# Padding the attention matmuls to 128 columns and fixing a finely interleaved order of all steps

## Chip, cores, metric

One core of a Trainium2 chip. The metric is the device time of one execution in microseconds. Each median below is that of three to seven executions of a kernel in one call. The calls ran on different chips; each had the kernel before beside the others, with a median of 174.8 to 175.2 us in every one. Engines: PE is the matrix engine, PEld its weight loads, DVE the vector engine, ACT the scalar engine, POOL the general-purpose one, SP the one that issues most DMAs.

Every run carries a label, fast or slow. A program on one core gets "slow" when it is over 1.5% above the fastest run of the same kernel in its call. Medians take all runs.

## The reference

Attention with polynomial features, then a Fourier mix with an MLP, in four batches:

```python
phi(x) = outer(S1 @ x, S2 @ x).reshape(64)      # q, k: (4, 4, 1088, 32) -> 64 features
kv  = einsum('bhsf,bhsd->bhfd', phi(k), v);  z = phi(k).sum(s)
x   = (phi(q) @ kv) / (phi(q) . z + 1e-6)       # heads joined: (4, 1088, 128)
u   = x + real(fft(fft(x, axis=1), axis=2))
out = u + relu(layernorm(u) @ w1) @ w2          # 128 -> 512 -> 128
```

## The kernel before

Three pieces matter. `pab` makes the two linear parts of the k features, `pnd` the numerators and denominators; both are fp32, and an fp32 matmul is two passes of PE in the trace. Each has a 128x128 stationary operand that is used once, and a short moving one (64 and 66 columns):

```python
# features of k, 4 of these per half batch
nc.tensor.matmul(_v(pab, 0, 128, 32 * j, [[256, 2], [1, 32]]),
                 self.kT[:, c0 : c0 + 128],
                 sblk[:].rearrange("p a h i -> p a (h i)"), start=True, stop=True, ...)
...
# numerators and denominators, 4 of these per step nd(c)
nc.tensor.matmul(_v(pnd, 0, 128, 132 * a + 66 * pr, [[1, 66]]),
                 self.qpT[:, pr, a, 32 + 128 * c : 160 + 128 * c],
                 kvz[:, pr, :], start=True, stop=True, ...)
```

The engines run in program order; the order is that of calls, each of which emits its PE, ACT and DVE work together:

```python
a1.pre_k(); ... a2.pre_k(); a1.nd(0); a2.pab(0); a1.nd(1); emit_table(3); a2.pab(1); ...
# tail: groups 2.0, 2.1, 3.0, 3.1 of the MLP and two remainders
m20.ln(); m21 = d2.bb(1); m20.tr(); m21.ln(); m20.m1(); m21.tr(); m20.m2()
m30 = d3.bb(0); m21.m1(); m30.ln(); m21.m2(); m31 = d3.bb(1); m30.tr(); ...
```

All ReLUs and PSUM copies of the MLP are on ACT. There are two PSUM buffers for the residual `pu`, so a new `bb` waits for the copy-out `ot` of an older group.

## Time and profile before

| | before |
|---|---|
| median of 3 runs | 174.64 us |
| span of the profiled run | 172.7 us |
| PE busy / idle | 135.7 / 37.0 us |
| PE clock at 0.5 | 91.1 us, PE busy in 69.4 of them |
| mean granted clock | 0.736 |

The last rows are worked out from the trace: PE's busy stretches laid over the clock records, each of which says how long the clock was granted at 1.0 or at 0.5. The first record starts at 6.5 us. What lies before it counts as 1.0, but the warm-up matmuls there start 427 ns apart, as at 0.5 elsewhere (216 ns at 1.0), and the rows leave that out.

From the page of the kernel before: busy time by engine, then PE's busy share and the granted PE clock in tenths, in 40 slices of 4.3 us, then the chain of waits by engine.

```profile
PE 135.7 (79%) x1325; PEld 92.0 (53%) x1333; DVE 78.6 (46%) x230; ACT 67.6 (39%) x164; POOL 41.5 (24%) x86
PE   7848995998429497998669899968987777869760
PEclk9995699569955555589855999995899965555555
PE 51%; DVE 20%; ACT 15%; DMA 4%; issue 3%; another core or an unknown queue 1%; ACTq 1%; SPq 0%; DVEq 0%
```

PE is the busiest engine and half of the chain, but over more than half of the span its clock is at 0.5. The busy row alone does not show it: in slices 13 to 17, where attention of two batches overlaps, and in the last eight, PE is mostly busy and half as fast.

PE's timeline of the kernel before at 46 to 58 us (start, duration, engine, line, operation, operands, shapes, count of passes; in brackets the idle time before it and what ended it):

```profile
45.70 1.11 PE L351 MATMUL pnd<-kvz_93,qpT 128*128 128x66 f32 x8
50.57 1.97 PE L271 MATMUL pab<-sblk,kT 128*128 128x64 f32 x8 [3.76 <-DVE rc L363]
52.33 1.92 PE L351 MATMUL pnd<-kvz_93,qpT 128*128 128x66 f32 x8
54.15 1.97 PE L271 MATMUL pab<-sblk,kT 128*128 128x64 f32 x8
55.91 1.92 PE L351 MATMUL pnd<-kvz_93,qpT 128*128 128x66 f32 x8
```

The first group of eight runs at full clock. Then PE idles 3.76 us, the clock falls, and four groups run without a break for 7 us and do not bring it back.

Two stretches of the kernel before (busy us of each engine, counts, then the mean clock, DMA share and GB/s):

```profile
core 0: us, PE busy (x) PEld busy (x) DVE busy (x) ACT busy (x) POOL busy (x), PEclk, DMA share, GB/s
48.00:75.00 27.00, 20.72 (x116) 13.96 (x117) 12.45 (x26) 7.94 (x19) 5.66 (x9) 0.50 0.00 1
139.00:172.70 33.70, 22.70 (x127) 12.84 (x129) 10.24 (x43) 15.00 (x34) 0.00 (x0) 0.51 0.12 35
```

These two hold about 60 of the 91 us at half clock: attention with its tables, and the tail of the MLP.

### The profile page before, as it was taken

To read this page: it belongs to the slowest core of one execution; us is meant where nothing else is said; L and a number is where in the kernel's file an instruction comes from. 1 tells how busy PE (TensorE), PEld (TensorE's weight loads), DVE (VectorE), ACT (ScalarE), POOL (GpSimd) and SP (SyncE) were. 2 spreads that over 40 slices of the span, in tenths; PEclk is the share of its full clock that TensorE was granted. 3 is DMA by queue.
4 is the path that set the end of the run, shared out by engine and by line. 5 is a ranking of instruction groups with operands and counts; after the bars stand their busy time and mean duration, and the time that the engine had idled before them with its cause. 6 is when DMAs were issued, how large, how long until landed. Compare 5 with 4: busy or idle time off the path is not lost.

```text
span 172.7 us, 3373 instructions
## 1 busy us (share of the span) xinstructions
PE 135.7 (79%) x1325; PEld 92.0 (53%) x1333; DVE 78.6 (46%) x230; ACT 67.6 (39%) x164; POOL 41.5 (24%) x86
## 2 busy tenths in 40 slices
PE   7848995998429497998669899968987777869760
PEld 2244774695429363356459665746954426445240
DVE  3364458343546535026853643575241580643110
ACT  2012155254531315254361635245546353527640
POOL 8999500225002305110012041100443200000000
PEclk9995699569955555589855999995899965555555
DMA  5799997980000000000000202000021000110211
GB/s 154 161 192 207 172 252 95 257 130 4 0 4 4 0 0 0 0 4 0 4 0 0 61 6 58 4 0 0 21 62 45 4 12 17 48 47 17 61 30 46
DMA packets 27968, 9.40 MB, mean 54 GB/s; under 512 B 20400, under 2 KB 26928, under 8 KB 27952
## 3 DMA queue, kind: packets, MB, share of 16 engines
q1 hardware_dynamic: 26912, 8.66, 22.1%
q0 software_dynamic: 672, 0.26, 1.4%
q10 hardware_dynamic: 368, 0.27, 0.6%
q8 instruction: 10, 0.16, 0.4%
q14 instruction: 6, 0.05, 0.1%
HBM read 7.22 MB, written 2.23 MB: 55 GB/s over the span
## 4 chain that ended last, share of the span: by engine, by line
PE 51%; DVE 20%; ACT 15%; DMA 4%; issue 3%; another core or an unknown queue 1%; ACTq 1%; SPq 0%; DVEq 0%
PE pq L287 11%; PE pnd L351 7%; PE pu L435 7%; PE ph L424 5%; PE pz L454 5%; PE pab L271 5%; PE pkv L320 4%; DMA kin_80<-in_k_dram 3%; ACT ht L428 3%; DVE qT L264 3%; DVE kp L234 3%; DVE un L404 3%; DVE kT L260 2%; PE pz L456 2%; DVE stats L393 2%
## 5 line engine op out<-in xcount | busy, mean ns | idle before, releaser
L297 DVE TENSOR_TENSOR qpT<-pq,qa 128x512 f32<-128x512 f32 x16 | 11.1, 691 | 28.4 <-ACT qa L295 28.4
L428 ACT ACTIVATE ht<-ph 128x512 bf16<-128x512 f32 (+1 forms) x40 | 18.2, 541 | 9.0 <-PE ph L424 6.8
L287 PE MATMUL pq<-qT,wa 32*64 32x256 f32 (+1 forms) x192 | 14.7, 396 | 8.5 <-DVE rc L363 6.5
L424 PE MATMUL ph<-unT,w_b 128*128 128x512 bf16 (+1 forms) x36 | 13.4, 496 | 6.6 <-ACT unT L415 5.0
L295 ACT COPY qa<-pq 128x512 f32<-128x512 f32 (+1 forms) x20 | 10.2, 520 | 21.0 <-PE pq L287 20.8
L435 PE MATMUL pu<-w_b,ht 128*128 128x128 bf16 x128 | 15.4, 288 | 1.8 <-ACT ht L428 1.7
L271 PE MATMUL pab<-sblk,kT 128*128 128x64 f32 x64 | 11.5, 342 | 6.5 <-DVE rc L363 3.8
L435 PEld LDWEIGHTS <-ht 128*128 128x128 bf16 x136 | 12.7, 132 | 6.5 <-ACT ht L428 5.8
L271 PEld LDWEIGHTS pab<-sblk,kT 128*128 128x128 f32 x64 | 10.5, 251 | 7.9 <-DVE rc L363 3.9
L287 PE MATMUL pq<-qT,wb 32*64 32x256 f32 (+1 forms) x192 | 14.2, 386 | 0.0
L234 DVE TENSOR_TENSOR kp<-ka,pab 128x1024 f32<-128x1024 f32 x8 | 9.7, 1216 | 9.9 <-ACT ka L233 9.9
L393 DVE BATCH_NORM_STATS2 stats<-pu 128x6 f32<-128x128 f32 x32 | 8.8, 274 | 11.7 <-remote 6.0
L287 PEld LDWEIGHTS pq<-qT,wa 32*64 32x64 f32 x192 | 5.1, 145 | 11.4 <-DVE rc L363 6.0
L404 DVE TENSOR_SCALAR un<-pu,mv,rstd 128x128 bf16<-128x128 f32 x32 | 10.9, 404 | 0.3
L424 PEld LDWEIGHTS <-w_b 128*128 128x128 bf16 x40 | 4.9, 129 | 10.7 <-issue 10.1
L287 PEld LDWEIGHTS pq<-qT,wb 32*64 32x64 f32 x192 | 7.3, 154 | 3.2 <-issue 1.8
L205 ACT ACTIVATE tg<-tf 128x546 f32<-128x546 f32 (+1 forms) x6 | 3.6, 601 | 13.6 <-DVE tf L203 13.6
L363 DVE TENSOR_SCALAR rc<-pnd 128x8 f32<-128x8 f32 (+1 forms) x20 | 3.1, 155 | 11.8 <-PE pnd L351 10.5
L439 ACT COPY ot<-pu 128x512 f32<-128x512 f32 x8 | 4.7, 585 | 9.0 <-PE pu L435 9.0
L233 ACT COPY ka<-pab 128x128 f32<-128x128 f32 x8 | 2.1, 263 | 15.4 <-PE pab L271 15.4
L412 PE MATMUL put<-ident_b,un 128*128 128x128 bf16 x34 | 7.2, 276 | 0.8 <-DVE un L404 0.2
L164 PE MATMUL warm<-wdummy 128*128 128x512 bf16 x18 | 6.7, 542 | 1.2 <-DVE wdummy L117 1.2
(247 smaller groups left out, 250.3 us busy)
## 6 DMA issues: line engine op xcount, KB each, us to landing
out_dram<-ot SPq DMA_DIRECT2D x32, 64.0 KB, 2.0
qin_76<-in_q_dram SPq DMA_DIRECT2D x1, 544.0 KB, 6.1
qin_77<-in_q_dram SPq DMA_DIRECT2D x1, 544.0 KB, 5.4
qin_78<-in_q_dram SPq DMA_DIRECT2D x1, 544.0 KB, 5.6
qin_79<-in_q_dram SPq DMA_DIRECT2D x1, 544.0 KB, 5.0
vin_84<-in_v_dram SPq DMA_DIRECT2D x4, 128.0 KB, 3.5
kin_81<-in_k_dram SPq DMA_DIRECT2D x4, 128.0 KB, 3.3
vin_85<-in_v_dram SPq DMA_DIRECT2D x4, 128.0 KB, 5.3
```

The lines of the kernel that those rows point to most:

```text
L234: nc.vector.tensor_tensor(out=_v(kp, 0, m, 0, [[64, 4 * nj], [8, 8], [1, 8]]), in0=_v(ka, 0, m, 0, [[8, 4 * nj], [1, 8], [0, 8]]), in1=_v( ...
L271: nc.tensor.matmul(_v(pab, 0, 128, 32 * j, [[256, 2], [1, 32]]), self.kT[:, c0 : c0 + 128], sblk[:].rearrange("p a h i -> p a (h i)"), sta ...
L287: nc.tensor.matmul(pq[f0 : f0 + 64, g % 2, w, n * k : n * k + n], wt[32 * g : 32 * g + 32, :, :], qT[32 * g : 32 * g + 32, pr, c0 : c0 + n ...
L295: nc.scalar.copy(qa[:, :, 0 : n * np_], pq[:, :, 0, 0 : n * np_])
L297: nc.vector.tensor_tensor(out=qpT[:, prs[0], :, c0 : c0 + n], in0=pq[:, :, 1, 0:n], in1=qa[:, :, 0:n], op=MULT)
L351: nc.tensor.matmul(_v(pnd, 0, 128, 132 * a + 66 * pr, [[1, 66]]), self.qpT[:, pr, a, 32 + 128 * c : 160 + 128 * c], kvz[:, pr, :], start=T ...
L393: nc.vector.bn_stats(stats[:, :], pu[:, i, :])
L404: nc.vector.tensor_scalar(out=self.un[:, i, :], in0=pu[:, i, :], scalar1=mv[:, i, 0:1], scalar2=rstd[:, i : i + 1], op0=SUB, op1=MULT)
L424: nc.tensor.matmul(ph[:, c, 0:n], w1_b[:, 128 * cc : 128 * cc + 128], self.unT[:, 0:n], start=True, stop=True)
L428: nc.scalar.activation(out=self.ht[:, cc, 0:n], in_=ph[:, c, 0:n], func=ACT.Relu)
L435: nc.tensor.matmul(self.pu[:, i, :], self.ht[:, cc, 128 * i : 128 * i + 128], w2_b[:, cc, :], start=False, stop=(cc == 3), skip_group_chec ...
L454: nc.tensor.matmul(pz[:, par, 0:NK], xx[:, t, :], tab[:, t, par, :], start=(t == 0), stop=False)
```

## The change

The intent: longer streams for the short matmuls, and an order in which each engine meets its operands ready. Every piece becomes a named step (`pab2.0` is PE's part, `ka2.0` ACT's, `kp2.0` DVE's), and a fixed list of 373 names gives the order. The diff, cut to its core:

```diff
-    kvzs = [const.tile([128, 2, 66], FP32, ...)]
+    kvzs = [const.tile([128, 2, 128], FP32, ...)]        # columns 66..127 stay zero
+    sblk2 = _v(sblk, 0, 128, 0, [[32, 2], [0, 2], [1, 32]])   # each bank of features twice
...
-    nc.tensor.matmul(_v(pab, 0, 128, 32 * j, [[256, 2], [1, 32]]), kT..., sblk...)
+    nc.tensor.matmul(_v(self.ps, 0, 128, 32 * j, [[256, 2], [128, 2], [1, 32]]), lhsT, sblk2, ...)
-    nc.tensor.matmul(_v(pnd, 0, 128, 132 * a + 66 * pr, [[1, 66]]), qpT..., kvz[:, pr, :], ...)
+    nc.tensor.matmul(pnd[:, 2 * a + pr, :], qpT..., kvz[:, pr, :], ...)
...
+ORDER = """
+wm1 wm1 ... kT0.0 pkr0 pab0.0 kT0.1 ka0.0 kp0.0 pab0.1 qT0 ...
+... bb2.1 st2.1 tr2.0 ut2.0 rs2.1 un2.1 mh2.0.0 re2.0.0 mh2.0.1 re2.0.2 re2.0.1 re2.0.3 tr2.1 ut2.1
+mm2.0 ot2.0 mh2.1.0 mh2.1.1 bb3.0 st3.0 re2.1.1 ... mm2.1 ot2.1 bb3.1 st3.1 ..."""
+for name in ORDER.split():
+    step[name]()
```

Beside these: the transpose of k is in halves, `z` has three buffers instead of two, and ten ReLUs (`rd`), two copies `ud` and three copies `od` are on DVE instead of ACT. The extra columns of `pab` and `pnd` are read by nothing.

## The prediction

> **What bounds the kernel now.** 174.64 us; the profiled span is 172.7 us. The chain of waits gives PE 51% of the span, DVE 20%, ACT 15%, DMA 4%. Busy: PE 79%, DVE 46%, ACT 39%. PE is the limit, but not at its own speed: the mean granted clock is 0.736. In stretches of 3 us it is either 1.0 or 0.5: 0.5 at about 13-19, 30-38, 48-75, 86-95, 115-121 and from 140 to the end, near 90 us in all.
>
> The timeline shows why for the attention steps. From 50.6 to 58 us PE runs k-feature and numerator matmuls (pab, pnd) without a break, and the clock stays at 0.5. The same groups of 8 passes take 1.97 us there and 1.03-1.10 us at full clock: 245 and 128-136 ns a pass. The 128x128 fp32 weight load sets that pace, for the 64 or 66 moving columns are short; an estimate from two single loads at full clock (33 columns 106 ns, 128 columns 180 ns) is 0.78 ns a column, about 100 ns of loading per pass. So the array streams under half of the time, and I read the clock as not counting that as busy. Dense streaming (pz, pq, 69-75 us) does raise it. The Trainium skill ("TensorE: Matmul & The Clock Gate", Part 1) says that the clock is half until a window of about 3.4 us has been busy; the trace's two levels agree.
>
> **What the change does.**
> 1. Padding: pab 64 to 128 and pnd 66 to 128 moving columns. 64+128 passes whose stream doubles to about 107 ns (estimate: twice the column time). Because it overlaps the weight load of about the same length, I expect the pace to stay at 125-145 ns at full clock: cost 0-2 us in all. If it did not overlap, +53 ns x 192 = 10 us at full clock.
> 2. Clock: streaming then counts as busy. Stretch 48-75 holds about 20 us of PE work at half clock; full clock would save about 8 us, then DVE (11 of 20 us there) and ACT's tables limit. 13-19, 30-38, 86-95, 115-121 together about 7 us.
> 3. Order: PE idles about 37 us, 8 of them at the start. The timeline: 2 us at 27-29 (behind kp, qT on DVE), 5 us at 42-50 (sine tables), several at 84-90 (layer norm). Finer interleaving should recover about 6 us.
> 4. Tail, 138-172 us: about 7.3 us per MLP group at half clock, PE waiting 0.8 us for `ot` before the next `bb`. In the new order mm2.0, both mh2.1, bb3.0 and mm2.1 can follow without a gap, enough for full clock. About 4 us, uncertain.
> 5. Small: kT in halves starts pab 0.6 us earlier; a few ReLUs and copies (0.5-0.6 us each) go from ACT to DVE.
>
> Most lies on the critical path, as PE does. Sum: 8 + 7 + 6 + 4 + 0.6 - 1 = about 24 us, less what other waits eat: 22.
>
> **Prediction: 152.5 us, 8 in 10 within 143 to 164. Faster by over 2%: 0.91, within 2%: 0.06, slower: 0.03.**
>
> **What would show it right.** Mean clock 0.85 or more; full clock through most of 30-75 us; a group of 8 padded pnd passes at 1.0-1.15 us; PE idle falling; DVE share rising above 50%; PE still the first engine in the chain. Clock 1.0 in part of the last 30 us.
>
> **What would make it wrong.** Padded passes at 180 ns or more (load and stream do not overlap); the clock still at 0.5 in attention, because it follows idle gaps rather than streaming; the fixed order putting a step ahead of its operand, so that engines block one another; DVE becoming the limit.

## The result

| | before | after |
|---|---|---|
| median of 4 runs | 174.79 us | 140.28 us (139.43 to 141.96) |
| profiled span | 172.7 us | 138.7 us |
| PE busy / idle | 135.7 / 37.0 us | 108.0 / 30.7 us |
| clock at 0.5, PE busy in it | 91.1 us, 69.4 | 7.4 us, 3.1 |
| mean clock | 0.736 | 0.973 |

The ratio is 0.7997, with a 95% interval of 0.7939 to 0.8056. A ratio is the mean time of one kernel's fast runs over that of the other's of the same rounds, so not quite the ratio of these medians. The gain of 34.5 us is outside the predicted range on its good side: 22 us had been forecast.

The same lines of the page of the kernel after (slices of 3.5 us):

```profile
PE 108.0 (78%) x1324; PEld 73.8 (53%) x1333; DVE 84.7 (61%) x249; ACT 62.2 (45%) x149; POOL 41.0 (30%) x86
PE   6795898899769979967789999299798677767520
PEclk9999999999999999999999999959999999999995
PE 45%; DVE 28%; POOL 9%; ACT 9%; issue 4%; another core or an unknown queue 0%; POOLq 0%; ACTq 0%; DVEq 0%
```

PE is as large a share of a shorter span (78 against 79%). The clock row is what changed: one drop in the middle, and one at the end when PE has finished.

PE's timeline of the kernel after, for groups that answer to those above:

```profile
38.80 0.41 PE L357 MATMUL pq<-qT,wb 32*64 32x32 f32 x16
39.15 1.16 PE L280 MATMUL pab<-sblk,kT 128*128 128x128 f32 x8
41.39 1.13 PE L428 MATMUL pnd<-kvz_93,qpT 128*128 128x128 f32 x8 [1.08 <-DVE xf L451]
42.42 1.16 PE L280 MATMUL pab<-sblk,kT 128*128 128x128 f32 x8
```

A padded group takes 1.13 to 1.16 us with 128 columns, where one with 66 columns took 1.11 at full clock. The largest gap in this stretch is 1.08 us, not 3.76.

And the stretches with the same kinds of work: attention of batches 1 and 2 with the tables, and the tail.

```profile
core 0: us, PE busy (x) PEld busy (x) DVE busy (x) ACT busy (x) POOL busy (x), PEclk, DMA share, GB/s
39.00:56.00 17.00, 14.20 (x167) 9.61 (x160) 10.78 (x25) 8.23 (x22) 1.05 (x3) 1.00 0.01 2
101.00:138.70 37.70, 23.44 (x213) 13.29 (x208) 19.41 (x75) 16.71 (x43) 3.77 (x7) 0.95 0.14 40
```

By the profile the 34.0 us of span are 27.7 us of PE busy time and 6.3 us of PE idle time. At half clock, 66.3 us of PE busy time went away; at most half of that, 33 us, is what full clock saves, and about 5 us came back as other PE busy time. So the clock is the larger item. Who raised it, the padding or the order, the two traces cannot say: both changed at once.

### The profile page after: what moved, and what is told of

Same layout as the page of the kernel before. It is cut to its first block, busy times and chain, and to the rows that moved or that the text cites. A ratio compares the mean times of both kernels' runs of the same rounds, so it can differ in the third digit from the quotient of the medians.

```text
span 138.7 us, 3380 instructions
## 1 busy us (share of the span) xinstructions
PE 108.0 (78%) x1324; PEld 73.8 (53%) x1333; DVE 84.7 (61%) x249; ACT 62.2 (45%) x149; POOL 41.0 (30%) x86
## 4 chain that ended last, share of the span: by engine, by line
PE 45%; DVE 28%; POOL 9%; ACT 9%; issue 4%; another core or an unknown queue 0%; POOLq 0%; ACTq 0%; DVEq 0%
PE pq L357 11%; PE pnd L428 7%; DVE un L507 6%; PE pu L544 5%; PE pkv L397 5%; PE pz L572 5%; DVE stats L493 5%; DVE kp L290 4%; PE ph L529 4%; DVE mv L494 4%; POOL kq L177 3%; PE pz L574 2%; ACT qa L368 2%; DVE qT L342 2%; ACT ht L534 2%
## 5 line engine op out<-in xcount | busy, mean ns | idle before, releaser
L534 ACT ACTIVATE ht<-ph 128x512 bf16<-128x512 f32 (+1 forms) x30 | 14.8, 565 | 6.1 <-PE ph L529 3.9
L544 PE MATMUL pu<-w_b,ht 128*128 128x128 bf16 x136 | 10.7, 220 | 3.5 <-ACT ht L534 2.4
L529 PE MATMUL ph<-unT,w_b 128*128 128x512 bf16 (+1 forms) x34 | 9.0, 350 | 4.0 <-ACT unT L520 3.1
L357 PE MATMUL pq<-qT,wb 32*64 32x256 f32 (+1 forms) x192 | 11.4, 322 | 0.0
L544 PEld LDWEIGHTS <-ht 128*128 128x128 bf16 x136 | 8.0, 98 | 6.0 <-ACT ht L534 3.8
L280 PE MATMUL pab<-sblk,kT 128*128 128x128 f32 x64 | 9.0, 284 | 2.3 <-DVE kp L290 1.6
L499 ACT ACTIVATE rstd<-mv,bias_eps 128x4 f32<-128x4 f32 (+1 forms) x10 | 3.0, 297 | 17.1 <-DVE mv L494 17.1
L286 ACT COPY ka<-pab 128x128 f32<-128x128 f32 (+1 forms) x10 | 2.5, 254 | 13.6 <-PE pab L280 13.6
L539 DVE TENSOR_SCALAR ht<-ph 128x512 bf16<-128x512 f32 (+1 forms) x10 | 4.5, 482 | 5.7 <-PE ph L529 3.9
L514 PEld LDWEIGHTS <-un 128*128 128x128 bf16 x34 | 2.9, 96 | 8.5 <-DVE un L507 8.0
L451 DVE TENSOR_TENSOR xf<-pnd,rc 128x256 f32<-128x256 f32 x16 | 6.8, 424 | 0.7
```

The source lines that it names most:

```text
L280: nc.tensor.matmul(_v(self.ps, 0, 128, 32 * j, [[256, 2], [128, 2], [1, 32]]), lhsT, sblk2, start=True, stop=True, skip_group_check=True)
L357: nc.tensor.matmul(pq[f0 : f0 + 64, g % 2, w, n * i : n * i + n], wt[32 * g : 32 * g + 32, :, :], self.qT[32 * g : 32 * g + 32, pr, c0 : c ...
L514: nc.tensor.transpose(self.put[:, 128 * i : 128 * i + 128], self.un[:, i, :], ident_b[:, :])
L529: nc.tensor.matmul(ph[:, c, 0:n], w1_b[:, 128 * cc : 128 * cc + 128], self.unT[:, 0:n], start=True, stop=True)
L534: nc.scalar.activation(out=self.ht[:, cc, 0:n], in_=self.ph[cc // 2][:, cc % 2, 0:n], func=ACT.Relu)
L544: nc.tensor.matmul(self.pu[:, i, :], self.ht[:, cc, 128 * i : 128 * i + 128], w2_b[:, cc, :], start=False, stop=(cc == 3), skip_group_chec ...
```

## The experiments

Theory A is the prediction's: the clock counts streaming, the padding supplies it, the order only fills idle time. Its rival B: the order closes idle gaps, and that keeps the clock. After the first four runs a third took their place. Theory C: the clock falls after a window of 3.4 us with little streaming, and rises only after a window with much; the order prevents falls, the padding makes rises. All kernels gave correct results. "New order" in the table means all of the change but the padding: the order, the form (k in halves, a third `z`) and the ReLUs and copies on DVE.

| run | what | median us | mean of the fast runs | mean clock of its runs |
|---|---|---|---|---|
| before | | 174.79 | 175.05 | 0.74 (profiled) |
| after | | 140.28 | 139.99 | 0.96 |
| pad_only | padding, old order | 165.61 | 165.8 | 0.83 |
| order_only | new order, no padding | 145.68 | 143.3 (1 run) | 0.90 |
| pnd_unpadded | after, pnd at 66 | 144.13 | 143.9 | 0.92 |
| pad96 | after, 96 columns | 143.25 | 143.4 | 0.93 |
| pad192 | after, 192 columns | 145.78 | 145.4 | 0.96 |
| old_tail | after, old order in the tail | 148.38 | 147.8 | 0.88 |
| old_head | padded, new order only in the tail | 158.63 | 156.1 | 0.87 |
| act_only | after, nothing moved to DVE | 144.58 | 144.3 | 0.93 |
| old_order_unpadded | old order in the new form | 171.6 | 171.0 | 0.76 |
| old_order_fill | the same with 42 wide dummies | 162.9 | 162.9 | 0.83 |
| narrow_fill | the same with 42 narrow dummies | 176.13 | 174.8 | 0.73 |
| old_order_warm | padded, dummies in all stages | 154.08 | 152.6 | 0.98 |
| fill_gap | after, 87 us mended | 139.31 | 138.9 | 0.95 |
| fill_more | fill_gap with 16 dummies | 137.52 | 137.5 | 0.98 |
| fill_more_unpadded | fill_more, no padding | 143.49 | 141.2 | 0.93 |

### 1. Each half alone: order_only and pad_only

order_only is the kernel after with the two matmuls short again:

```diff
-    _v(self.ps, 0, 128, 32 * j, [[256, 2], [128, 2], [1, 32]]), lhsT, sblk2
+    _v(self.ps, 0, 128, 32 * j, [[256, 2], [1, 32]]), lhsT, sblk[:].rearrange(...)
-    pnd[:, 2 * a + pr, :], ..., kvz[:, pr, :]
+    pnd[:, 2 * a + pr, 0:66], ..., kvz[:, pr, 0:66]
```

> The kernel after with its order and all else, but pab streams 64 and pnd 66 columns again. Theory A (the clock counts streaming, padding supplies it): the clock falls to 0.5 again through most of the attention stretches, mean clock 0.72 to 0.85, time 153 to 165 us. Theory B (the new order closes the idle gaps, and that keeps the clock): mean clock 0.93 or more, time within 3 us of 140.3. Groups of 8 pnd passes at full clock should take 1.03 to 1.10 us as in the padded kernel, so no gain from shorter streams.

pad_only is the kernel before with the padded matmuls (and the strides of `rc` and `xf` that go with them), its order kept.

> The kernel before with its order and all else, but pab and pnd padded to 128 columns. Theory A: mean clock above 0.90, stretch 48-75 us at full clock, time 150 to 158 us. Theory B: clock stays at 0.70 to 0.80 as the idle gaps remain, time 171 to 177 us. If padding also costs PE time where the clock is low, the time would be above 175.

Measured: 145.7 and 165.6 us. Neither theory holds as stated, though the one fast run of order_only, 143.3 us, is at the edge of B's range (its clock, 0.915, is under it). The order alone gains 29 us of the 34.5, the padding alone 9. Against the one fast run of the kernel before in that call, 170.3 us, these are 27.0 and 4.5 us, so the padding alone is worth less than its median says; on top of the order, padding adds 5.4 us by medians, 3.3 by fast runs. PE's busy share and the clock of order_only, then of pad_only:

```profile
PE   6937999799769988966899999838979675867640
PEclk9995599999965599998557999995999999999955
```

```profile
PE   7757997797749185998659799969897767857750
PEclk9997589999656978599995999996999995795555
```

Without padding the new order still has three drops before the end, each two or three slices long (its trace: 6.8 to 10.2 us; a fourth is one window). With padding the old order has eight drops where the kernel before has six, but four of them, at 59, 66, 86 and 110 us, last one window of 3.4 us; the kernel before has none under 6.8 us and one of 27. So a drop and a rise have different causes. That gave theory C.

### 2. Which matmul: pnd_unpadded

> The kernel after with pab padded and pnd at 66 columns. pnd is 128 of the 192 padded passes. Theory A: about two thirds of what order_only loses, mean clock 0.78 to 0.90, time 147 to 158 us. Theory B: no change, 139 to 143 us.

`pab` stays padded, `pnd` has 66 columns. 144.1 us: just above B's range (fast runs: 143.9 against 140.0 of the kernel after), and A's 147 is not reached. The result is near that of order_only, so `pnd`, two thirds of the padded passes, carries most of the padding's share; the difference to order_only is within the spread of runs.

### 3. The tail and the head: old_tail and old_head

> The kernel after, but from the first remainder group on (after the last numerator step) all four engines follow the order of before, with all ReLUs and copies on ACT. If the order of the tail made its clock: 0.5 over the last 30 us again, time 145 to 150 us. If the tail keeps full clock because it starts with it: clock 0.9 or more in the tail, time 141 to 144 us.

The list of steps was cut at the first remainder group; the old calls, written as steps, took the place of one part.

```diff
-ORDER = new head + new tail
+ORDER = new head + old tail        # old_tail
+ORDER = old head + new tail        # old_head
```

old_tail took 148.4 us, 8.1 more than the kernel after. Its tail starts at full clock and loses it:

```profile
core 0: us, PE busy (x) PEld busy (x) DVE busy (x) ACT busy (x) POOL busy (x), PEclk, DMA share, GB/s
101.00:146.90 45.90, 31.54 (x228) 18.22 (x231) 16.36 (x66) 20.12 (x56) 4.69 (x8) 0.71 0.13 37
```

Against the kernel after, whose tail from the same moment has a clock of 0.95 and lasts 37.7 us, that is the whole loss. So a good head is not enough to keep the tail's clock. But old_tail changes two things: it also has the tail's eight ReLUs and three copies back on ACT. act_only (section 7) has these on ACT in the new order, and takes 41.0 us from 101 us on at a clock of 0.83. So, by these profiles, about 3.3 of the 8.2 us belong to these moves, and 4.9 to the order.

> Padded, with the order of before up to the last numerator step and the new order of the tail. If head and tail add up: pad_only (165.6) less what the new tail gave in old_tail against the kernel after (148.4 - 140.3 = 8.1), so 156 to 159 us. If the gain of the tail hangs on the clock that the head leaves: 161 to 166 us.

158.6 us, two runs at 156.1 and two at 161.2. Head (158.6 - 140.3 = 18.3) and tail (8.1) add to 26.4, near the 25.3 between pad_only and the kernel after (by fast runs 16.1 + 7.8 = 23.9 against 25.8): they add up within the spread.

### 4. What the clock counts: old_order_fill and narrow_fill

Here the old order, without padding, gets dummy matmuls ahead of six stalls of PE; they compute nothing that is used.

```diff
+... wm6 q0.0 ... wm8 q1.0 ... wm4 kt1 ... wm12 pab2.0 ... wm8 q2.0 ... wm4 pbr1   # wmN: N dummies
```

> The order of before in the form of the kernel after, without padding, with 42 dummy 512-column matmuls ahead of six stalls of PE in the first 70 us (before q0.0, q1.0, kt1, pab2.0, q2.0, pbr1). They do no useful work. Theory C: drops at 13, 30 and 47 us go away, stretch 13-75 us is at full clock, time 160 to 168 us against about 175. If the gain of the new order is idle time filled with useful work and not the clock: 173 to 178 us.

> old_order_fill with its 42 dummies (bf16, 512 columns[...]) replaced by 42 fp32 dummies with a 128x128 weight load and 16 columns: two passes of about 130 ns, so the same occupancy of PE, but streaming about a tenth of it. Theory C (share of streaming): the clock drops at 13, 30 and 47 us as without dummies, mean clock 0.70 to 0.78, time 170 to 177 us. If the clock follows PE being occupied, not streaming: as old_order_fill, 161 to 165 us, mean clock 0.81 or more.

Measured: 162.9 and 176.1 us; the same kernel without dummies took 171.6. Forty-two useless matmuls gain 8.7 us when they are wide; when they are narrow, they lose 4.5 us (by fast runs 8.1 gained, 3.9 lost). The timeline of old_order_fill around one of the stalls, then of narrow_fill:

```profile
40.53 2.75 PE L191 MATMUL warm<-wdummy 128*128 128x512 bf16 x12
43.97 1.10 PE L280 MATMUL pab<-sblk,kT 128*128 128x64 f32 x8 [0.69 <-DVE kT L338]
45.40 1.22 PE L429 MATMUL pnd<-kvz,qpT 128*128 128x66 f32 x8 [0.33 <-DVE xf L452]
```

```profile
48.75 4.77 PE L266 MATMUL narrow<-ident_f 128*128 128x16 f32 x24
53.35 1.95 PE L289 MATMUL pab<-sblk,kT 128*128 128x64 f32 x8
55.09 1.92 PE L438 MATMUL pnd<-kvz,qpT 128*128 128x66 f32 x8
```

After the wide ones a `pab` group takes 1.10 us, after the narrow ones 1.95. And narrow_fill's page shows that occupancy is not it, with PE busier than in any other run here:

```profile
PE 149.6 (86%) x1409; PEld 106.9 (61%) x1417; DVE 79.6 (46%) x234; ACT 67.6 (39%) x164; POOL 42.0 (24%) x86
PEclk9985597559965555579955899995799965555555
```

One stretch of narrow_fill leaves no gap to blame: from 24 to 31 us PE is busy all the time. The window from 25.4 to 28.8 us is at full clock with a streaming share of 0.35 (counted as below), and behind it the clock falls (columns as above: stretch, length, busy us of PE first, mean clock third from the end).

```profile
24.00:31.00 7.00, 7.00 (x90) 6.59 (x88) 5.64 (x10) 3.68 (x10) 0.00 (x0) 0.84 0.93 166
```

The time and the clock decide for streaming against occupancy. The two kinds of dummies differ in data type too, but padded fp32 passes raise the clock as well (pad_only: 48.6 to 52.0 us, share 0.94, then full clock). What the threshold is can be read over all traces. For each clock window of 3.41 us I estimated the share of streaming: over the matmul passes that start in it, moving columns, times two for fp32, divided by the granted clock (2.4 columns per ns at 1.0) and weighted by rows over 128, over 3.41 us. The 2.4 GHz is the Trainium skill's ("TensorE: Matmul & The Clock Gate", opening table), and the trace agrees: wide dummies of 512 columns start 216 ns apart at 1.0 and 427 at 0.5; the factor of two for fp32 agrees with pad192 below. In 17 traces:

| clock in the window | share of streaming | windows | the next window |
|---|---|---|---|
| 1.0 | under 0.35 | 65 | 64 fell to 0.5 |
| 1.0 | 0.35 to 0.5 | 85 | 8 fell |
| 1.0 | 0.5 and more | 396 | none fell |
| 0.5 | under 0.7 | 93 | 3 rose to 1.0 |
| 0.5 | 0.7 to 0.8 | 28 | 10 rose |
| 0.5 | 0.8 and more | 49 | 42 rose |

So there are two thresholds, about 0.35 to stay and about 0.75 to come back. This table was made after the fact and its weights are mine. A second count has 66, 86, 394, 104, 29 and 48 windows in these rows; 65, 7 and 0 fell, and 3, 11 and 41 rose. By PE's busy share in place of streaming there is no such cut: of 520 windows at 1.0 with half or more busy 47 fell, and of 107 at 0.5 with 0.8 or more busy 52 stayed low. The table explains the runs: by the same count, windows of short `pab` and `pnd` groups alone reach 0.48 at half clock, far too little to return, and at full clock about 0.41 (66 columns take 55 ns of a pass of 135), hardly enough to stay. Padded, they reach 0.94 and more at half clock, and return. Idle time inside a window of such groups then makes the fall, and it need not be one long gap: in 18 of the 65 windows of the second count no gap reached 0.8 us.

### 5. The cost of padding: pad96 and pad192

> The kernel after with pab and pnd padded to 96 columns instead of 128. The traces so far suggest theory C: the clock drops after a window of 3.4 us in which under about 0.35 of the time was streaming, and rises again only after a window with about 0.75 or more; order prevents drops, padding makes rises. At half clock 96-column passes stream about 0.65 to 0.7 of the time, under the second threshold: after a drop the clock should stay low nearly as long as in order_only. Theory C: 142 to 146 us, mean clock 0.87 to 0.94, pnd groups of 8 still 1.03 to 1.10 us at full clock. If any streaming counts in proportion: halfway to the padded kernel or better, 141 to 143 us.

> The kernel after with pab at 192 columns and three of each four pnd matmuls at 192. If the weight load of 100 to 110 ns hides behind the stream, a pass costs the longer of the two: about 160 to 170 ns at full clock (2 x 192 columns / 2.4 per ns) against 135, groups of 8 at 1.3 us, about 176 passes x 30 ns = 5 us of PE, of which 3 to 5 on the time: 143 to 146 us. If load and stream add: 135 at 128 columns would already hold both, and 192 would add 53 ns a pass: 147 us or more.

143.3 us with 96 columns, at a clock of 0.93, is in theory C's range and 0.3 us above the other's, less than its runs differ (142.7 to 144.4). Its trace has only one drop in attention, so this run does not tell the readings apart. Groups with 96 and with 192 columns (six of the eight passes have 192, two 128), at full clock:

```profile
39.02 1.10 PE L429 MATMUL pnd<-kvz,qpT 128*128 128x96 f32 x8 [0.85 <-ACT kvz L421]
```

```profile
38.74 1.43 PE L429 MATMUL pnd<-kvz,qpT 128*128 128x192 f32 x8 [0.85 <-ACT kvz L421]
40.70 1.57 PE L280 MATMUL pab<-sblk,kT 128*128 128x192 f32 x8
42.94 1.44 PE L429 MATMUL pnd<-kvz,qpT 128*128 128x192 f32 x8 [0.67 <-DVE xf L452]
```

In the groups shown, 66 columns take 1.11 us, 96 1.10, 128 1.13 and 192 1.44. Over these whole traces eight `pnd` passes at full clock take 1.00 to 1.11 us with 66 columns, 1.03 to 1.13 with 96 and 1.05 to 1.16 with 128. Up to 128 the stream is hidden and the length is nearly free; beyond it each pass pays: (1.44 - 1.13) / 6 = 52 ns for 64 more columns, 0.81 ns a column (2 / 2.4 is 0.83). pad192 costs 5.5 us against the kernel after at a clock as high, as the first reading had it. The first expectation of step 1 of the prediction holds. At half clock the length is free too: 1.92 us with 66 columns in the kernel before, and 1.91 with 128 at 91.8 us in the kernel after.

### 6. The clock alone in the old order: old_order_warm and a control

> The order of before, padded, with 82 dummy matmuls ahead of the stalls of PE in all stages. It asks what the old order would take if the clock never fell. Theory C with the clock as the main thing: mean clock above 0.92, time 148 to 154 us, so most of the 25 us that the new order gains on pad_only (165.6) is clock and the rest, 8 to 14 us, is idle time filled. If the order gains mainly by filling idle time: the clock rises but the time stays at 156 us or more.

> Control: the order of before, unpadded, in the form of the kernel after (kT in halves, three z buffers, separate steps). Expected within 1% of the kernel before: 173.5 to 176.5 us. A larger difference would mean that the form, not the order, carries part of the gain.

(The count in the first is wrong: the kernel has 87 dummies.) The control took 171.6 us, 2% less than the kernel before, not within 1%. By fast runs it is 171.0 against 172.3 us, 0.7% less, which is within it. So 1 to 3.5 us may belong to the form of the kernel (k in halves, a third `z`) or to where windows fell; this stays open.

old_order_warm took 154.1 us, 152.6 in its fast runs, at a clock of 0.98. Its clock row, with two short drops before the end:

```profile
PEclk9999999999879959999999999999999999999995
```

So the old order, padded, gains 11.5 us by medians and 13.2 by fast runs over pad_only when its clock is held. Its form is that of the kernel after, so the 1 to 3.5 us above may be in this; that leaves 8 to 12 us for the clock. What is left to the kernel after, 12.6 to 13.8 us at the same clock, is the order itself: operands ready in time, less idle PE that must be waited out, and the work moved to DVE. It is an upper bound, for some dummies also delay real work. Of the 25 us that the kernel after gains over pad_only, then, 8 to 12 us are clock, at most 12.6 to 13.8 us order and the moves to DVE, and the rest may be form.

### 7. ReLUs and copies on DVE: act_only

```diff
-rd1.0.0 ... ud1.1 ... od1.1 ... rdr0.3 ... odr1
+re1.0.0 ... ut1.1 ... ot1.1 ... rer0.3 ... otr1      # all on ACT, same places
```

> The kernel after with its ten ReLUs and five copies on DVE (rd, ud, od steps) back on ACT in the same order. Expected: a small loss, 140.5 to 143 us; if they carry much of the gain of the tail, 144 us or more.

144.6 us: 4.3 more than the kernel after (by fast runs too), over the expected small loss and in the range of the second reading, that they carry much of the gain of the tail. The kernel after takes 37.7 us from 101 us on at a clock of 0.95; act_only:

```profile
101.00:142.00 41.00, 25.61 (x206) 14.80 (x202) 15.14 (x63) 20.26 (x55) 3.08 (x6) 0.83 0.13 38
```

So all of the 3.3 us between the two profiled spans is in the tail. PE's longest waits in the kernel after, then in act_only (who waited for whom, us in total, times, longest):

```profile
PE put L514 <- DVE un L507: 3.6, 3, 2.3
PE ph L529 <- ACT unT L520: 3.1, 4, 0.9
PE pu L544 <- ACT ht L534: 2.4, 4, 1.2
```

```profile
PE pu L544 <- ACT ht L534: 4.1, 8, 1.3
PE pu L594 <- ACT ot L551: 3.5, 2, 2.2
PE ph L529 <- ACT unT L520: 3.5, 5, 0.9
```

With all of them on ACT, its ReLUs hold PE twice as often, and its copy `ot` holds PE for 2.2 us at a time. act_only also has 17.4 us at half clock against 7.4, so part of the 4.3 us comes by the clock.

### 8. A better version: fill_gap, fill_more, fill_more_unpadded

> The kernel after with 14 steps around 87 us in another order: normalise group 1.0 before the statistics of 1.1, and kc3, kt3, kz3 and nd3.0 ahead of the group's first matmul. PE waits 2.3 us there in the kernel after, and the clock drops for 3.4 us behind it. Expected: that gap under 1 us, no drop at 90 us, 1.5 to 3 us less than the kernel after: 137.3 to 139 us. If DVE limits there instead: within 1 us of 140.3.

The kernel after has one drop in the middle, behind a gap of 2.3 us at 87 us. There, DVE does the statistics of group 1.1 before normalising 1.0:

```profile
core 0: us, PE busy (x) PEld busy (x) DVE busy (x) ACT busy (x) POOL busy (x), PEclk, DMA share, GB/s
86.90:90.30 3.40, 0.88 (x6) 0.42 (x6) 3.19 (x15) 0.59 (x3) 0.00 (x0) 1.00 0.00 0
90.30:93.70 3.40, 3.06 (x19) 2.73 (x20) 1.23 (x4) 1.60 (x4) 0.00 (x0) 0.50 0.00 0
```

```diff
-bb1.1 rs1.0 st1.1 un1.0 kc3 rs1.1 un1.1 tr1.0 kt3 ut1.0 kz3 mh1.0.0 nd3.0 rc3.0
+bb1.1 rs1.0 kc3 un1.0 kt3 kz3 st1.1 tr1.0 ut1.0 nd3.0 rc3.0 rs1.1 un1.1 mh1.0.0
```

In fill_gap the same moment has no gap:

```profile
86.19 0.70 PE L411 MATMUL pt<-ident_f,kvT 33*64 33x33 f32 x8 [0.15 <-ACT kvT L403]
86.82 1.06 PE L514 MATMUL put<-ident_b,un 128*128 128x128 bf16 x4
87.75 1.13 PE L428 MATMUL pnd<-kvz,qpT 128*128 128x128 f32 x8
```

Its time is 139.3 us, 1.0 less, at the edge of both expectations, and its runs (138.0 to 140.2) overlap those of the kernel after, so this is no clear gain: the gap went, but in the profiled run another window, at 109 us in the tail, fell below the threshold. So it was tried with 16 dummies ahead of five more stalls (`wm6` before pab0.1, three before each of mh2.0.0 and mh3.0.0, two before each of tr2.1 and tr3.1).

> fill_gap with 16 dummy matmuls ahead of five stalls (before pab0.1, mh2.0.0, tr2.1, mh3.0.0, tr3.1), so that no window of the tail falls under a third of streaming. Expected: no drop before the last 8 us, time 137.0 to 138.5 us, and less spread from run to run. If dummies delay real work: 139 us or more.

137.5 us, all four runs within 137.05 to 137.84, clock 0.98: 2.8 us less than the kernel after and the fastest, with a narrower spread. By fast runs it is 1.8% less, under the 2% that counts as faster here, and the two ran in different calls: a small gain. Its trace has no drop before 130.7 us, where fill_gap had one at 112.7, so the dummies held the clock of the tail. Which of the five places helped was not tested.

> fill_more (137.5 us) without padding. If padding serves the clock alone and the dummies and order hold it: 137 to 140 us with mean clock above 0.96. If drops in attention at about 40 and 65 us, where there are no dummies, remain: 140 to 144 us with mean clock 0.90 to 0.95.

143.5 us by median, 141.2 by fast runs, with 10 us at half clock from 39.6 us on in its trace. The second reading holds: in attention after the first 12 us, where these kernels have no dummies, padding still keeps the clock. Padding and order are not two ways to the same thing.

## Why the prediction was wrong

The time was outside the range; the mechanism of the padded passes was right, and two terms of the sum were not.

- **Step 1, cost of padding, 0 to 2 us: right.** 1.13 us a group against 1.11; the crossover past 128 columns was shown by pad192. The estimate of the load alone, from single loads, was loose in its source: of the three single 128-column loads of about 180 ns, two (14.5 and 66.7 us) fell at half clock, and the third, at 4.7 us, before the first record, among passes as slow as at half clock. The figure itself stands: the first load after a pause at full clock takes 186 ns in the same trace (at 9.0 and 23.3 us).
- **Step 2, clock, 8 + 7 us from the padding: the step that failed.** The prediction took the padding for what supplies the clock ("Streaming then counts as busy"). pad_only gains 9 us (4.5 against the fast run) and still has 53 us at half clock. Streaming is what counts, as narrow_fill shows, but half clock in this kernel begins behind windows in which little streams, most often for idle time among short matmuls, which padding does not fill. Padding shortens the stay at half clock. The size of the whole clock item was too small as well: with step 4 it was 19 us, where 66 us of PE busy time left half clock, up to 33 us. For 48 to 75 us I let DVE and the tables take over after 8 us; about the same work (and 33 more short `pq` passes) took 17 us instead of 27. Stage by stage (up to 48, 75, 127 us and the end of the kernel before; 39, 56, 101 us and the end of the kernel after; about the same work) the profiled span lost 9, 10, 7 and 8 us. The prediction had 8 for the second, 4 for the last and 13.6 for the other two, so the shortfall is spread: 2 us, 4 us and 2.4 us.
- **Step 3, order, 6 us of idle time: right in size as idle time (6.3 us), wrong as the value of the order.** The order alone gains 29 us, since it also keeps windows of 3.4 us above the threshold, and since operands that come in time matter even at full clock (12.6 to 13.8 us at most, by old_order_warm).
- **Step 4, tail, about 4 us: right for the order alone, half of the whole.** old_tail shows 8.1 us, of which the order is about 4.9. The clock went as described: 0.95 in the new order, 0.71 in the old.
- **Step 5, ReLUs and copies on DVE, counted within 0.6 us: too small.** act_only shows 4.3 us, part of it by the clock; 3.3 us of the profiled spans' difference lie in the tail.
- **DVE share above 50%, PE first in the chain, mean clock over 0.85, full clock in most of 30 to 75 us, groups at 1.0 to 1.15 us:** all seen (61%, 45%, 0.97, all of it, 1.13 to 1.16).

Left open: how the 12.6 to 13.8 us of the order at equal clock divide into single steps; the 1 to 3.5 us of the kernel's form; and the exact weights of the clock's count (rows, transposes), for which the table is an estimate.

## What to carry to other kernels

Lay PE's timeline over its clock before costing anything: at half clock, busy time is not work, and every step that brings the clock back is worth half of the PE time behind it. Guard against the fall with order (or, where order cannot, with wide dummy matmuls in stalls), and make short matmuls as long as their weight load hides, so that a fall can be over after one window (four of eight in pad_only, none of six in the kernel before). Judge an order with its clock, for the two cannot be read apart from one trace: run the old order with the clock held, and the new one without its help.

## What the Trainium skill lacked or had wrong

- "TensorE: Matmul & The Clock Gate", Part 1, says that activity sets the clock and that a busy window of about 3.4 us raises it and an idle one lowers it. The window agrees: all clock records here but the last of each trace, which is cut short, last whole multiples of 3.41 us. Missing, but for a remark on transposes in Part 4, is what counts as busy: with PE 86% busy but narrow streams (narrow_fill) the clock was 0.72 to 0.75; with wide dummies in the same places it was 0.81 to 0.84.
- The same page, the table of "Why this matters for your kernels", advises no idle gap over about 3 us. Here shorter ones were enough when little else streamed in the window: 2.3 us at 87 us in the kernel after, none of 0.8 us in 18 of 65 windows that ended in a fall, and no gap at all in narrow_fill from 25.4 us. (Part 1 tells of a kernel whose frequent short idle times made the clock swing, without a size.) The estimate from 17 traces is a share of 0.35 to stay at full clock and 0.75 to return; the page has no such pair.
- The same page, Part 3, "What overlaps and what doesn't", says that weight loads overlap matmuls in flight only where the row group differs (Part 2, and Part 3 a few lines above, also name a background buffer). Full 128-row fp32 loads did hide the stream here: 1.11 us for eight passes of 66 columns, 1.13 of 128, 1.44 once six of them had 192.
- No page has the pace of fp32 matmuls with a load for each: 135 to 145 ns a pass at full clock and 239 at half clock (1.91 us for eight) as the mean of a group of eight, 112 and 214 ns from one pass to the next within it, up to 128 columns; 0.81 ns for each further column.
